# Softmax and memory denominators made by VectorE alone, in an attention and feed-forward kernel

## The chip, the cores and the metric

The kernel runs on one core of a Trainium2 chip. The metric is the device time of one execution in microseconds (us). A core has five engines with a queue of their own each, and each queue is worked off strictly in its order: TensorE (PE, with its weight loads as PEld), VectorE (DVE), ScalarE (ACT), GpSimd (POOL) and SyncE (SP, which issues the DMAs here). Engines wait for each other by semaphores.

## The reference

Four batches, eight heads, 576 rows, head size 64. Each head has causal softmax attention and a lookup in a memory matrix, mixed by a gate; the result goes through a feed-forward network with a rational activation.

```python
scores = scale * np.matmul(q, k.transpose(0, 1, 3, 2))      # causal mask, minus the row's maximum
a = np.exp(scores)
a /= a.sum(-1, keepdims=True) + 1e-09
local = np.matmul(a, v)
q_p = phi(q)                                   # phi(x) = x + 1 above zero, exp(x) below
mem_ret = np.einsum('bhsd,bhde->bhse', q_p, M_prev)
mem_norm = np.einsum('bhsd,bhd->bhs', q_p, z_prev)[..., None] + 1e-06
g = 1.0 / (1.0 + np.exp(-beta))[None, :, None, None]
attn_out = g * mem_ret / mem_norm + (1 - g) * local
# x = attn_out as [2304, 512]
h = x @ w_in                                   # 512 -> 2048
P = a0 + a1 * h + a2 * h**2 + a3 * h**3
Q = 1.0 + abs(b0) * abs(h) + abs(b1) * h**2
out = (P / (Q + 1e-6)) @ w_out                 # 2048 -> 512
```

The two weights arrive as 64-bit floats, everything else as 32-bit floats. The change concerns the two denominators: `sum + 1e-9` of the softmax and `phi(q).z + 1e-6` of the memory.

## The kernel before

The attention is cut into 16 units, one for each batch and pair of heads (`prep`, `scores`, `tile23`, `tail`, `av`). A unit has nine softmax tiles: for each of its two heads four of 128 rows with 128, 256, 384 and 512 keys, and one for the last 64 rows of both heads together, with 576 keys. The function `prob` (lines 697 to 724) makes one such tile: VectorE takes the row's maximum (L704), ScalarE the exponential with its row sum (L708), then the row sum is turned into a factor and the tile is scaled by it, and TensorE transposes it (`tr`, L503). The factor has the gate in it: `(sum + 1e-9) * 1/(1 - g)`, and then its reciprocal (L719). The tile called st holds the statistics of one softmax tile, one number for each row: columns for the maxima, the sums, the product and the reciprocal. The constants g1 and gtail hold 1/(1 - g).

In `prep` each unit makes phi(q) (the tile E), the product with z (written over nk), its sum over the head (den, 128 x 10, L655), and from it the factor `g / (phi(q).z + 1e-6)`, with which E is scaled (L662, recorded under the helper's L519 or L520). Here GpSimd adds 1e-6 (L657), VectorE takes the reciprocal (L658), and GpSimd or VectorE multiplies by g (the constant gt).

The feed-forward part takes 256 rows at a time and six of the sixteen blocks of the hidden width beside the attention, the other ten after it. Its chain `act_chain` runs on ScalarE, GpSimd and VectorE. The weights are split into a high and a low part on the three engines as well (L981 to L1000).

The order of all instructions is made ahead of time by a planner in the kernel's file (`Sched.place`). Each operation has a cost in nanoseconds for each engine that may do it; the planner repeatedly picks the operation that can start first by its own clock, with priorities to break ties, and where several engines may do an operation it takes the one with the smallest sum of start and cost. The costs are `c_pool`, `c_dve` and the like. A table RATE stretches an operation on VectorE or GpSimd while the other runs an operation of certain kinds (the letter at the end of an entry, "-" for none). So a cost that changes in one place moves instructions everywhere on all engines. The softmax factor had two choices:

```python
sc.op([("pool", c_pool(1, 1), lambda: G.tensor_scalar(...), "s"),          # L716
       ("dve", 130, lambda: V.tensor_scalar(...))],                        # L717
```

The planner put 90 of the 144 on GpSimd (L716) and 54 on VectorE (L717).

Of the kernel before, what the change touches and what calls it, by code (L numbers as in the profile page):

```python
# [15 lines left out]
ALU = mybir.AluOpType  # L16
# [28 lines left out]
def c_act(n, psum=True, ap=0):  # L45
    return (51 if psum else 93) + 0.833 * n + 93 * ap


def c_dve(n):
    return 69 + 1.042 * n  # L50


def c_dve1(n):
    return 69 + 0.64 * n


def c_pool(n, ap=0):
    return 161 + 0.833 * n + 83 * ap


def c_pool2(n):
    return 55 + 2.39 * n
# [254 lines left out]
def tile_attention_ffn(  # L317
# [15 lines left out]
    V, A, G, T, SY = nc.vector, nc.scalar, nc.gpsimd, nc.tensor, nc.sync  # L333
# [11 lines left out]
    sc = Sched()  # L345
# [27 lines left out]
    for i in range(2):  # L373
        r, r2 = slice(64 * i, 64 * i + 64), slice(64 - 64 * i, 128 - 64 * i)
# [9 lines left out]
    bt = const.tile([128, H], F32, name="bt")  # L384
    SY.dma_start(out=bt, in_=beta.partition_broadcast(128))
    gt = const.tile([128, H], F32, name="gt")
# [43 lines left out]
    for x in tags(atp, "qd", N["qd"], [128, 2, 128], F32R):  # L430
        for i in range(2):
            r = slice(64 * i, 64 * i + 64)
# [73 lines left out]
    def act(cost, fn, reads, writes, pri):  # L506
        return sc.op([("act", cost, fn)], reads, writes, pri)

    def dve(cost, fn, reads, writes, pri, kind="-"):
        return sc.op([("dve", cost, fn, kind)], reads, writes, pri)  # L510

    def pool(cost, fn, reads, writes, pri):
        return sc.op([("pool", cost, fn, "s")], reads, writes, pri)

    def tt(n, out, in0, in1, op, reads, writes, pri, engines=("pool", "dve")):

        def kw():
            return dict(out=out(), in0=in0(), in1=in1(), op=op)
        opts = {"pool": ("pool", c_pool2(n), lambda: G.tensor_tensor(**kw()), "t"),  # L519
                "dve": ("dve", c_dve(n), lambda: V.tensor_tensor(**kw()), "2")}  # L520
        return sc.op([opts[e] for e in engines], reads, writes, pri)
# [89 lines left out]
    def prep(u, p):  # L611
        bb, c = divmod(u, KC)
# [13 lines left out]
        for i in range(2):  # L626
            r = slice(64 * i, 64 * i + 64)
# [11 lines left out]
        for i in range(0 if d["direct"] else 2):  # L639
            o = d["qk"][i]  # L640
            r = slice(64 * i, 64 * i + 64)
# [6 lines left out]
        E, R, den = sc.buf("E"), nk, sc.buf("den")  # L648
# [5 lines left out]
           [(E, None), (zb, None)], [(R, None)], p)  # L654
        dve(c_dve(640), lambda: V.tensor_reduce(out=den.t, in_=R.t, axis=AX.X, op=ALU.add),  # L655
            [(R, None)], [(den, None)], p)
        pool(c_pool(10), lambda: G.tensor_scalar(den.t, den.t, 1.0, 1e-6, op0=ALU.mult, op1=ALU.add), [], [(den, None)], p)  # L657
        dve(140, lambda: V.reciprocal(den.t, den.t), [], [(den, None)], p)  # L658
        tt(10, lambda: den.t, lambda: den.t, lambda: gt[:, 2 * c:2 * c + 2].unsqueeze(1).to_broadcast([128, 5, 2]), ALU.mult,
           [], [(den, None)], p)  # L660

        tt(640, lambda: E.t, lambda: E.t, lambda: den.t.unsqueeze(3).to_broadcast([128, 5, 2, 64]), ALU.mult, [(den, None)], [(E, None)], p)  # L662

        bk, tf = bank(), bank()
# [32 lines left out]
    def prob(Pst, parts, gcol, n, p):  # L697

        P, st = Pst
        mx = len(parts) - 1  # L700
        for x, (bk, w, m, c0) in enumerate(parts):
            def f(bk=bk, w=w, m=m, x=x):
                s = bk.t[:, 0:w]
                V.tensor_tensor_reduce(out=s, in0=s, in1=m, scale=-0.125, scalar=st.t[:, 0:1] if x else 3.0e38,  # L704
                                       op0=ALU.add, op1=ALU.min, accum_out=st.t[:, x:x + 1])
            dve(c_dve(w) + 8, f, [(st, ("m", 0))] if x else [], [(bk, None), (st, ("m", x))], p)
        for x, (bk, w, m, c0) in enumerate(parts):
            act(c_act(w, ap=2), lambda bk=bk, w=w, x=x, c0=c0: A.activation(  # L708
                P.t[:, c0:c0 + w], bk.t[:, 0:w], AF.Exp, bias=st.t[:, mx:mx + 1], scale=-1.0, accum_out=st.t[:, 2 + x:3 + x]),
                [(bk, None), (st, ("m", mx))], [(P, x), (st, ("l", x))], p)  # L710
        l = slice(2, 3)
        if mx:
            l = slice(3, 4)
            dve(65, lambda: V.tensor_tensor(out=st.t[:, 3:4], in0=st.t[:, 2:3], in1=st.t[:, 3:4], op=ALU.add),
                [(st, ("l", 0))], [(st, ("l", 1))], p, "2")
        sc.op([("pool", c_pool(1, 1), lambda: G.tensor_scalar(st.t[:, 4:5], st.t[:, l], 1e-9, gcol, op0=ALU.add, op1=ALU.mult), "s"),  # L716
               ("dve", 130, lambda: V.tensor_scalar(st.t[:, 4:5], st.t[:, l], 1e-9, gcol, op0=ALU.add, op1=ALU.mult))],  # L717
              [(st, ("l", mx))], [(st, "r")], p)
        dve(75, lambda: V.reciprocal(st.t[:, 5:6], st.t[:, 4:5]), [(st, "r")], [(st, "i")], p)  # L719
        sc.op([("pool", c_pool(n, 1), lambda: G.tensor_scalar(P.t[:, 0:n], P.t[:, 0:n], st.t[:, 5:6], 0.0, op0=ALU.mult, op1=ALU.add), "s"),  # L720
               ("act", c_act(n, False, 1), lambda: A.activation(P.t[:, 0:n], P.t[:, 0:n], AF.Copy, scale=st.t[:, 5:6])),
               ("dve", c_dve1(n) + 61, lambda: V.tensor_scalar(P.t[:, 0:n], P.t[:, 0:n], st.t[:, 5:6], None, op0=ALU.mult), "1")],
              [(st, "i")], [(P, None)], p)
        return P

    def scores(u, i, t, p):
        bb, c = divmod(u, KC)
        d = ST[u]
        n = 128 * (t + 1)
        bk = bank()  # L730
        qs = slice(128 * t, 128 * t + 128)

        def f():
            if d["direct"]:
                r, x = slice(64 * i, 64 * i + 64), d["t"].t[:, 0:4 * SM].rearrange("p (a b) -> p a b", a=4)
                return [(x[r, a, qs], x[r, b, 0:n]) for a, b in ((1, 2), (1, 3), (0, 2))]
            x = d["qk"][i].t
            return [(x[:, 0, qs], x[:, 1 + b, 0:n]) for b in range(2)]
        m, src = (3, d["t"]) if d["direct"] else (2, d["qk"][i])
        P = probs(n)  # L740
        mm(lambda: [(bk.t[:, 0:n], a, b, x == 0, x == m - 1) for x, (a, b) in enumerate(f())], (6 if d["direct"] else 2) * c_mm(n),
           [(src, None)], [(bk, None)], p, take=P)
        return prob(P, [(bk, n, mk[:, 512 - 128 * t:640], 0)], g1[:, 2 * c + i:2 * c + i + 1], n, p)
# [43 lines left out]
    def tail(u, p):  # L787
# [12 lines left out]
        mm(lambda: f(s1, SM, 2 * SM, 3 * SM), 3 * c_mm(SM), [(t, None), (qd, None)], [(s1, None)], p, take=P)  # L800
        mm(lambda: f(s2, 64, 4 * SM, 4 * SM + 64), 3 * c_mm(64), [(t, None), (qd, None)], [(s2, None)], p)
        P = prob(P, [(s1, 512, mk[:, 0:512], 0), (s2, 64, mt, 512)], gtail[:, c:c + 1], S, p)
        pt, p2 = bank(), bank()
        tr(lambda: [(b4(pt)[:, x, :], P.t[:, 128 * j:128 * j + 128], idf) for x, j in enumerate((3, 0, 1, 2))], 4 * 109,
# [103 lines left out]
    pr = PRI  # L908
    load(0, -1)
    prep(0, 0)  # L910
    for u in range(U):
        base = 100.0 * u
        if u + 1 < U:
            load(u + 1, base + pr["load"])
        for i in range(2):
            tiles01(u, i, base + 10 + pr["head"] * i)
            av(u, i, 0, base + pr["av0"] + pr["head"] * i)
        if u + 1 < U:
            prep(u + 1, base + pr["prep"])
        for i in range(2):  # L920
            for t in range(2, 4):
                tile23(u, i, t, base + pr["t2"] + pr["head"] * i + 4 * (t - 2))
        tail(u, base + pr["tail"])
        for i in range(2):
            av(u, i, 1, base + pr["av1"] + i)
        spill(u, base + pr["av1"] + 2)
# [169 lines left out]
    for g in range(NG1):  # L1096
        t0 = 256 * g
        p = FP + pr["group"] * g
# [47 lines left out]
    for g in range(NG1 - turns + 1):  # L1146
        ts = [256 * x for x in (range(turns) if g == 0 else [g + turns - 1])]
        t0 = ts[0]
        p = FP2 + 5000 * (t0 // 256)
        ob = group(ts, list(range(F0, NF)), "h2", "o2", None, "xg2", p, pr["ahead2" if g < NG1 - turns else "last"])  # L1150
        for ti in range(2 * len(ts)):
            r = t0 + 128 * ti
# [68 lines left out]
```

## Time and profile before

| | us |
|---|---|
| three runs: lowest, median, highest | 733.32, 734.24, 737.19 |
| the profiled execution | 736.42 |
| its span, first to last instruction | 734.6 |

| engine | busy us | share of the span |
|---|---|---|
| TensorE | 664.3 | 90% |
| VectorE | 590.4 | 80% |
| ScalarE | 506.5 | 69% |
| GpSimd | 461.4 | 63% |

The attention's last softmax tile is scaled at about 360 us; after that only feed-forward work is left. The busy share is a mean over these two very different parts. A row of groups gives the busy time of all instructions of a line, operation and shape, the mean of one in ns, and the idle time of the engine in front of them. The chain of work is followed back from the last instruction to what released each step, so its pieces are the time on the path that ended last.

### The profile page before, as it was taken

Reading aid. Unit: us, or ns where it says so; the run is one execution under the profiler, and the core shown is the slowest. Engines: PE = TensorE matmul, PEld = TensorE weight load, DVE = VectorE, ACT = ScalarE, POOL = GpSimd, SP = SyncE. Lnnn points to the kernel's source line nnn. Section 1 sums busy time; section 2 is a strip of 40 time slices with the busy share of each in tenths; the row PEclk is TensorE's granted clock in tenths of the full one; section 3 lists DMA queues with packets and bytes.
Section 4 is the critical chain, followed back from the end, with each engine's and each line's share of the span. In section 5 each row is a group of like instructions: output and inputs, shape, how many; then the busy total and the mean of one; then the engine's idle time right before and its main releaser. Section 6 shows DMA issues by size and latency. Waiting matters only on the chain.

```text
span 734.6 us, 12896 instructions
## 1 busy us (share of the span) xinstructions
PE 664.3 (90%) x4113; PEld 578.9 (79%) x4113; DVE 590.4 (80%) x1371; ACT 506.5 (69%) x1121; POOL 461.4 (63%) x558
## 2 busy tenths in 40 slices
PE   3778788998989998889999999878899999999997
PEld 2656567887886777679889998767798998998996
DVE  5787877798999998789789999899775766657674
ACT  3756778789988899879666686575463854755762
POOL 3566656767765786656545887777753745645663
PEclk9999999999999999999999999999999999999999
DMA  6888687846679766764275443612342212212102
GB/s 152 178 202 216 138 204 180 235 112 191 157 168 236 188 162 157 219 159 104 80 260 161 169 159 106 242 61 87 116 124 91 72 62 83 87 58 72 45 9 79
DMA packets 102580, 102.56 MB, mean 140 GB/s; under 512 B 67632, under 2 KB 80432, under 8 KB 100208
## 3 DMA queue, kind: packets, MB, share of 16 engines
q1 hardware_dynamic: 102512, 101.73, 49.7%
q8 instruction: 33, 0.54, 0.3%
q14 instruction: 35, 0.29, 0.1%
HBM read 52.27 MB, written 23.59 MB: 103 GB/s over the span
## 4 chain that ended last, share of the span: by engine, by line
PE 51%; DVE 17%; ACT 11%; DMA 8%; issue 4%; POOL 4%; SPq 4%; DVEq 0%; ACTq 0%; POOLq 0%
PE bk L492 48%; SPq L485 4%; DMA xf<-in_moe_w_in_dram 3%; PE bk L503 3%; DVE bk L704 2%; ACT Ps L708 2%; DVE g L545 2%; ACT P L708 1%; DVE bk L525 1%; DVE gh L525 1%; ACT g L539 1%; DVE bk L987 1%; POOL tw L519 1%; DVE wa L983 1%; DVE wu L990 1%
## 5 line engine op out<-in xcount | busy, mean ns | idle before, releaser
L492 PEld LDWEIGHTS bk<-xg,w2i 128*128 128x128 f32 x1080 | 133.7, 193 | 6.5 <-DVE gl L1038 1.9
L492 PE MATMUL bk<-xg,w2i 128*128 128x256 f32 x1080 | 135.0, 284 | 3.3 <-DVE gl L1038 1.7
L492 PE MATMUL bk<-w2o,gh 128*128 128x512 f32 x360 | 113.3, 396 | 2.9 <-DVE gl L1038 2.9
L1014 ACT ACTIVATE ta<-bk 128x512 f32<-128x512 f32 x72 | 42.9, 596 | 86.7 <-PE bk L492 84.6
L1018 POOL TENSOR_SCALAR tw<-ta,cb 128x512 f32<-128x512 f32 x60 | 48.5, 808 | 83.5 <-ACT ta L1014 83.3
L519 POOL TENSOR_TENSOR tw<-tw,gh 128x512 f32<-128x512 f32 x54 | 70.6, 1307 | 40.6 <-DVE gh L525 39.6
L519 POOL TENSOR_TENSOR tw<-tw,ta 128x512 f32<-128x512 f32 x68 | 89.3, 1316 | 3.8 <-ACT tw L1019 0.3
L492 PE MATMUL bk<-xg,w1i 128*128 128x256 f32 x648 | 84.0, 284 | 0.2
L704 DVE CUSTOM_DVE_ANT_0 bk<-bk,mk 128x512 f32<-128x512 f32 (+3 forms) x144 | 72.7, 518 | 13.4 <-PE bk L492 11.9
L492 PEld LDWEIGHTS bk<-xg,w1i 128*128 128x128 f32 x648 | 80.9, 191 | 2.5 <-DVE g L545 0.8
L492 PEld LDWEIGHTS bk<-w2o,gh 128*128 128x128 f32 x360 | 67.1, 191 | 15.9 <-DVE gl L1038 3.1
L492 PE MATMUL bk<-w2o,gl 128*128 128x512 f32 x180 | 71.6, 398 | 5.7 <-DVE gl L1038 5.7
L1023 DVE TENSOR_TENSOR tb<-bk,tb 128x512 f32<-128x512 f32 x72 | 49.3, 684 | 33.0 <-ACT tb L1015 31.6
L1022 ACT ACTIVATE ta<-tw,lnb 128x512 f32<-128x512 f32 x72 | 52.0, 724 | 32.1 <-POOL tw L519 28.3
L492 PE MATMUL bk<-qk 128*128 128x128 f32 (+3 forms) x256 | 65.5, 360 | 4.3 <-DVE g L545 1.2
L492 PE MATMUL bk<-w1o,gh 128*128 128x512 f32 x216 | 68.7, 399 | 0.0
L525 DVE SCALAR_TENSOR_TENSOR gh<-bk,ca,ta 128x512 fp32r<-128x512 f32 x72 | 53.5, 743 | 18.4 <-ACT ta L1027 15.3
L525 DVE SCALAR_TENSOR_TENSOR bk<-bk,ca,tw 128x512 f32<-128x512 f32 x72 | 54.1, 751 | 14.4 <-POOL tw L519 13.9
L1015 ACT ACTIVATE tb<-bk,ca 128x512 f32<-128x512 f32 x72 | 55.7, 775 | 0.1
L1025 DVE SCALAR_TENSOR_TENSOR bk<-tb,ca,bk 128x512 f32<-128x512 f32 x72 | 53.8, 748 | 1.9 <-ACT ta L1014 1.0
L716 POOL TENSOR_SCALAR st<-st,g 128x1 f32<-128x1 f32 x78 | 24.0, 308 | 48.7 <-ACT Ps L708 41.4
L708 ACT ACTIVATE Ps<-bk,st 128x128 f32<-128x128 f32 (+2 forms) x96 | 46.0, 483 | 10.9 <-DVE st L704 8.1
(152 smaller groups left out, 1623.4 us busy)
## 6 DMA issues: line engine op xcount, KB each, us to landing
qk<-tt SPq DMA_DIRECT2D x32, 384.0 KB, 4.8
xh<-xg SPq DMA_DIRECT2D x9, 1024.0 KB, 4.7
xg<-xh SPq DMA_DIRECT2D x9, 1024.0 KB, 4.8
xf<-in_moe_w_in_dram SPq DMA_DIRECT2D x16, 512.0 KB, 4.4
qk<-tt SPq DMA_DIRECT2D x32, 256.0 KB, 3.6
xf<-in_moe_w_out_dram SPq DMA_DIRECT2D x16, 512.0 KB, 4.8
xs<-x SPq DMA_DIRECT2D x16, 288.0 KB, 2.7
xf<-xs SPq DMA_DIRECT2D x9, 512.0 KB, 5.8
```

What stands on the lines that cost most here:

```text
L485: SY.dma_start(out=o, in_=i)
L492: T.matmul(o, lhsT=l, rhs=r, start=s0, stop=s1, skip_group_check=more)
L519: opts = {"pool": ("pool", c_pool2(n), lambda: G.tensor_tensor(**kw()), "t"), "dve": ("dve", c_dve(n), lambda: V.tensor_tensor(**kw()), "2")}
L525: return dve(c_dve(n) + 61 * ap, lambda: V.scalar_tensor_tensor(out=out(), in0=in0(), scalar=scalar() if callable(scalar) else scalar, in1 ...
L704: V.tensor_tensor_reduce(out=s, in0=s, in1=m, scale=-0.125, scalar=st.t[:, 0:1] if x else 3.0e38, op0=ALU.add, op1=ALU.min, accum_out=st.t ...
L708: act(c_act(w, ap=2), lambda bk=bk, w=w, x=x, c0=c0: A.activation(P.t[:, c0:c0 + w], bk.t[:, 0:w], AF.Exp, bias=st.t[:, mx:mx + 1], scale= ...
L1014: act(c_act(N), lambda: A.activation(a_(), h(), AF.Abs), [(hb, None)], [(ta, None)], p)
L1015: sc.op([("act", c_act(N, ap=2), lambda: A.activation(b_(), h(), AF.Identity, scale=ca[:, 3:4], bias=ca[:, 2:3])), ("dve", c_dve(N) + 61, ...
L1018: sc.op([("pool", c_pool(N, 2), lambda: G.tensor_scalar(w_(), a_(), cb[:, 1:2], cb[:, 0:1], op0=ALU.mult, op1=ALU.add), "s"), ("act", c_ac ...
L1022: act(c_act(N, False, 1), lambda: A.activation(a_(), w_(), AF.Ln, scale=2.0 ** -63, bias=lnb[:, 0:1]), [(tw, None)], [(ta, None)], p)
L1023: dve(c_dve(N), lambda: V.tensor_tensor(out=b_(), in0=h(), in1=b_(), op=ALU.mult), [(hb, None)], [(tb, None)], p)
L1025: dve(c_dve(N) + 61, lambda: V.scalar_tensor_tensor(out=h(), in0=b_(), scalar=ca[:, 1:2], in1=h(), op0=ALU.add, op1=ALU.mult), [(tb, None) ...
```

## The change

Both denominators become one VectorE operation of the form (a + constant) * b, where b is a second tile: 1/(1 - g) for the softmax, and for the memory the constant bt, which holds 1/g. The multiplication by g after the reciprocal falls away. GpSimd has no part in either. In the planner the operation costs 75 ns for the softmax and 90 ns for the memory, of kind "-".

```diff
-        pool(c_pool(10), lambda: G.tensor_scalar(den.t, den.t, 1.0, 1e-6, op0=ALU.mult, op1=ALU.add), [], [(den, None)], p)
+        dve(90, lambda: V.scalar_tensor_tensor(
+            out=den.t, in0=den.t, scalar=1e-6, in1=bt[:, 2 * c:2 * c + 2].unsqueeze(1).to_broadcast([128, 5, 2]), op0=ALU.add,
+            op1=ALU.mult), [], [(den, None)], p)
         dve(140, lambda: V.reciprocal(den.t, den.t), [], [(den, None)], p)
-        tt(10, lambda: den.t, lambda: den.t, lambda: gt[:, 2 * c:2 * c + 2].unsqueeze(1).to_broadcast([128, 5, 2]), ALU.mult,
-           [], [(den, None)], p)
...
-        sc.op([("pool", c_pool(1, 1), lambda: G.tensor_scalar(st.t[:, 4:5], st.t[:, l], 1e-9, gcol, op0=ALU.add, op1=ALU.mult), "s"),
-               ("dve", 130, lambda: V.tensor_scalar(st.t[:, 4:5], st.t[:, l], 1e-9, gcol, op0=ALU.add, op1=ALU.mult))],
-              [(st, ("l", mx))], [(st, "r")], p)
+        dve(75, lambda: V.scalar_tensor_tensor(out=st.t[:, 4:5], in0=st.t[:, l], scalar=1e-9, in1=gcol, op0=ALU.add, op1=ALU.mult),
+            [(st, ("l", mx))], [(st, "r")], p)
```

In the changed file the softmax's operation stands on L715, its reciprocal on L717, the memory's operation on L657 and its reciprocal on L660; the scaling on GpSimd is L718, the maximum L703. TensorE has the same 4040 matrix instructions in both orders, VectorE 1481 instructions in place of 1373, GpSimd 450 in place of 563, ScalarE 952 in place of 963.

The first place is GpSimd's queue in the first unit, from the product with z (nk) on. Before:

```order
L519 TENSOR_TENSOR nk_129<-E_155,zb_154 128x640
L657 TENSOR_SCALAR den_156<-den_156 128x10
L519 TENSOR_TENSOR den_156<-den_156,gt 128x10
L519 TENSOR_TENSOR E_155<-E_155,den_156 128x640
L716 TENSOR_SCALAR st_164<-st_164,gtail 128x1
L720 TENSOR_SCALAR P_157<-P_157,st_164 128x576
L531 TENSOR_SCALAR w1i_187<-tw_217 128x512
```

And with the change (P and Ps are softmax tiles, w1i a weight's high part):

```order
L519 TENSOR_TENSOR nk_129<-E_155,zb_154 128x640
L519 TENSOR_TENSOR E_155<-E_155,den_156 128x640
L531 TENSOR_SCALAR w1i_187<-tw_217 128x512
L519 TENSOR_TENSOR w1i_193<-tw_217,w1i_187 128x512
L718 TENSOR_SCALAR Ps_162<-Ps_162,st_166 128x256
```

The three small operations on den and st are gone from GpSimd, and the scaling of this first tile went to ScalarE.

The second place is VectorE's queue in the eleventh unit, from the sum of den (L655) on, at about 230 us of the trace before. Before:

```order
L655 TENSOR_REDUCE den_156<-nk_129 128x10
L719 RECIPROCAL st_167<-st_167 128x1
L704 ISA bk_120,st_164<-bk_120,mk 128x512
L704 ISA st_164 128x1
L658 RECIPROCAL den_156<-den_156 128x10
L719 RECIPROCAL st_168<-st_168 128x1
L520 TENSOR_TENSOR den_156<-den_156,gt 128x10
L704 ISA bk_124,st_166<-bk_124,mk 128x512
L704 ISA st_166 128x1
L719 RECIPROCAL st_169<-st_169 128x1
L717 TENSOR_SCALAR st_164<-st_164,g_100 128x1
```

With the change:

```order
L655 TENSOR_REDUCE den_156<-nk_129 128x10
L715 SCALAR_TENSOR_TENSOR st_170<-st_170,g_100 128x1
L715 SCALAR_TENSOR_TENSOR st_169<-st_169,g_100 128x1
L657 SCALAR_TENSOR_TENSOR den_156<-den_156,bt 128x10
L717 RECIPROCAL st_170<-st_170 128x1
L717 RECIPROCAL st_169<-st_169 128x1
L660 RECIPROCAL den_156<-den_156 128x10
L703 ISA bk_122,st_168<-bk_122,mk 128x512
L703 ISA st_168 128x1
L525 SCALAR_TENSOR_TENSOR bk_126<-bk_126,ca,tw_218 128x512
```

Three of the new operations stand in front of three reciprocals, and the next tile's maximum (bk_122) stands behind all six.

The third place is GpSimd's queue at the same point. Before:

```order
L519 TENSOR_TENSOR nk_129<-E_155,zb_154 128x640
L716 TENSOR_SCALAR st_167<-st_167,g_100 128x1
L716 TENSOR_SCALAR st_168<-st_168,g_100 128x1
L657 TENSOR_SCALAR den_156<-den_156 128x10
L720 TENSOR_SCALAR Ps_163<-Ps_163,st_167 128x384
L716 TENSOR_SCALAR st_169<-st_169,g_100 128x1
L720 TENSOR_SCALAR P_157<-P_157,st_168 128x512
L519 TENSOR_TENSOR E_155<-E_155,den_156 128x640
```

With the change:

```order
L519 TENSOR_TENSOR nk_129<-E_155,zb_154 128x640
L718 TENSOR_SCALAR Ps_162<-Ps_162,st_167 128x256
L718 TENSOR_SCALAR P_157<-P_157,st_170 128x512
L718 TENSOR_SCALAR P_158<-P_158,st_169 128x512
L519 TENSOR_TENSOR E_155<-E_155,den_156 128x640
L519 TENSOR_TENSOR tw_217<-tw_217,ta_211 128x512
```

The small operations between the wide ones are gone; a wide operation follows a wide one.

## Rows read from the trace of the kernel before

**Rows 1.** The page: busy us of each engine, then the chain's shares.
```profile
PE 664.3 (90%) x4113; PEld 578.9 (79%) x4113; DVE 590.4 (80%) x1371; ACT 506.5 (69%) x1121; POOL 461.4 (63%) x558
PE 51%; DVE 17%; ACT 11%; DMA 8%; issue 4%; POOL 4%; SPq 4%; DVEq 0%; ACTq 0%; POOLq 0%
```

**Rows 2.** Busy time in stretches: stretch, its length, then each engine's busy us.
```profile
core 0: us, PE busy (x) PEld busy (x) DVE busy (x) ACT busy (x) POOL busy (x), PEclk, DMA share, GB/s
...
150.00:300.00 150.00, 136.26 (x892) 116.78 (x892) 137.86 (x420) 134.47 (x360) 103.18 (x150) 0.98 0.69 172
...
360.00:550.00 190.00, 178.17 (x1108) 159.72 (x1107) 168.91 (x250) 116.77 (x189) 130.96 (x121) 0.98 0.43 148
```

**Rows 3.** What TensorE waited for: us in total, times, longest us.
```profile
PE bk L492 <- DVE gl L1038: 10.3, 5, 2.9
PE bk L503 <- POOL Ps L720: 7.7, 7, 2.0
...
PE bk L503 <- POOL E L519: 4.6, 2, 4.2
```

**Rows 4.** Groups by shape on GpSimd: count, busy us, mean ns, idle before.
```profile
L716 POOL TENSOR_SCALAR st<-st,g 128x1 f32<-128x1 f32 x78 | 24.0, 308 | 48.7 <-ACT Ps L708 41.4 <-ACT P L708 2.3 <-DMA qk<-tt 0.8
...
L657 POOL TENSOR_SCALAR den<-den 128x10 f32<-128x10 f32 x16 | 3.4, 210 | 5.0 <-DVE den L655 2.3 <-DVE st L719 1.8
L716 POOL TENSOR_SCALAR st<-st,gtail 128x1 f32<-128x1 f32 x12 | 3.2, 264 | 11.0 <-DVE st L714 10.7
...
L519 POOL TENSOR_TENSOR den<-den,gt 128x10 f32<-128x10 f32 x11 | 2.4, 221 | 2.2 <-DVE den L658 1.2 <-DVE st L719 0.8
```

**Rows 5.** Groups by shape on VectorE.
```profile
L525 DVE SCALAR_TENSOR_TENSOR bk<-bk,ca,tw 128x512 f32<-128x512 f32 x72 | 54.1, 751 | 14.4 <-POOL tw L519 13.9
...
L525 DVE SCALAR_TENSOR_TENSOR tw<-tw,gh 128x512 f32<-128x512 f32 x18 | 17.0, 948 | 0.1
...
L717 DVE TENSOR_SCALAR st<-st,g 128x1 f32<-128x1 f32 x50 | 10.0, 206 | 3.6 <-ACT Ps L708 2.3 <-ACT P L708 0.7
...
L714 DVE TENSOR_TENSOR st<-st 128x1 f32<-128x1 f32 x16 | 5.6, 348 | 1.4 <-ACT P L708 1.3
...
L520 DVE TENSOR_TENSOR den<-den,gt 128x10 f32<-128x10 f32 x5 | 2.3, 453 | 0.0
```

**Rows 6.** Lines L714 and L717: ns of the shortest, median and longest.
```profile
L714 DVE TENSOR_TENSOR st<-st x16: 142/159/1206, 18.2 to 344.0; 128x1 f32<-128x1 f32 x16
...
L717 DVE TENSOR_SCALAR st<-st,g x50: 187/205/216, 20.5 to 357.4; 128x1 f32<-128x1 f32 x50
```

**Rows 7.** Order of time near 281 us: start us, duration us, engine, operation.
```profile
281.30 1.27 POOL L519 TENSOR_TENSOR ms<-mn,ms 128x512 fp32r<-128x512 f32 x1
...
281.50 1.09 DVE L714 TENSOR_TENSOR st<-st 128x1 f32<-128x1 f32 x1
```

**Rows 8.** Pieces of the chain that ended last: start us, us, what.
```profile
31.59 0.23 DVE st L717 x2
...
54.29 0.36 POOL st L716
54.66 0.11 issue
...
258.41 0.66 DVE st L714
...
281.57 1.02 DVE st L714
...
313.21 0.21 DVE st L717
...
347.67 0.27 POOL st L716
```

**Rows 9.** Groups by shape on VectorE that the planner moves.
```profile
L722 DVE TENSOR_SCALAR Ps<-Ps,st 128x384 f32<-128x384 f32 x2 | 2.9, 1426 | 0.0
...
L520 DVE TENSOR_TENSOR w2o<-wu,w2o 128x512 fp32r<-128x512 f32 x1 | 1.8, 1783 | 0.0
```

## The prediction

> **What bounds the kernel now.** I read the page's busy shares and chain first, then the busy time by stretches, then TensorE's waits, then the groups of the small operations that the change touches. TensorE is busy 664.3 us of 734.6 and makes 51% of the chain that ended last; VectorE is second with 17%, GpSimd has 4% [rows 1]. So time is lost where TensorE waits, and the engine most often waited for is VectorE, not the one that is relieved. The mean hides the middle of the attention: from 150 to 300 us VectorE is busy 137.86 of 150 us, more than TensorE (136.26), while GpSimd has 103.18 [rows 2]. VectorE has 12.1 us to spare there, GpSimd 46.8. The change puts work on the fuller of the two. What speaks for it is that TensorE waits 7.7 us for scaled softmax tiles and 4.6 us for the scaled E, both from GpSimd [rows 3], behind chains that cross between the engines.
>
> **The change part by part.** *Removed.* GpSimd loses 78 and 12 operations of L716, 16 of L657 and 11 products with gt: 24.0 + 3.2 + 3.4 + 2.4 = 33.0 us of busy time [rows 4]. Most of it costs nothing today, since GpSimd has room. On the path lie eight pieces of L716, 2.6 us together (the first 0.36, the last 0.27 us [rows 8]), and three pieces on den, 0.21, 0.22 and 0.34 us, 0.8 together, near their groups' means [rows 4]. With each of these eleven goes one crossing between engines, 0.11 us by the piece after the first [rows 8], 1.2 us in all. VectorE loses 54 operations of L717, of which 13 lie on the path in twelve pieces, 2.0 us together (first 0.23 for two, last 0.21) [rows 8]. What goes from the path: 2.6 + 0.8 + 1.2 + 2.0 = 6.6 us.
>
> *Added.* VectorE gets 144 + 16 = 160 operations with two tiles in SBUF as inputs, and the order shows that none stays on GpSimd. No row of before has this operation at 128x1. The nearest is L714: same tile st, same size, right behind the same row sum, also two inputs in SBUF. Undisturbed it takes 142 to 159 ns, but its longest takes 1206 and its mean is 348 [rows 5, 6]. L717, which takes the gate as a scalar for each row and reads one tile, never takes more than 216 ns in 50 [rows 6]. The difference is a wait for GpSimd: one L714 starts at 281.50 us while GpSimd is inside an operation of 1.27 us begun at 281.30, and ends at 282.59, within 0.02 us of GpSimd's end [rows 7]. That the new form of operation suffers the same way is seen at a larger size: with both inputs in SBUF (tw, gh) it has a mean of 948 ns, with one in PSUM (bk) 751, though the number of elements is the same [rows 5]. 948 - 751 = 197 ns and 348 - 159 = 189 ns: two operations, one price, 0.19 us a piece in the mean.
>
> The Trainium skill, SBUF — State Buffer, section Who interferes with whom, says that a VectorE instruction with two SBUF inputs contends with a GpSimd instruction that reads SBUF, and that whichever came second is blocked until the first has finished, while one with at most one SBUF input outside the two-port modes is free of it. By that rule all 160 new operations are exposed and the 54 replaced ones were not; the rows on L714 and L717 agree. Without the rule one could hold the new 128x1 form for an operation like L717, and the sum would then be the lower bound below.
>
> *What of it lies on the path.* Two of the 16 L714 lie on the chain, with 0.66 and 1.02 us [rows 8]: 1.68 / 16 = 0.105 us of path per operation. 160 x 0.105 = 16.8 us. The sum: 16.8 - 6.6 = +10.2 us. From below: if the new operation never waited and came on the path as L717 does, 2.0 / 54 = 0.037 us each, it would be 5.9 - 6.6 = -0.7 us. From above: the product on den, L520, also with two inputs in SBUF, has a mean of 453 ns [rows 5], a stall of 294 in place of 189; 16.8 x 294 / 189 = 26.1, and the sum is +19.5 us. I take +10, since L714 is the nearer row by place, size and count.
>
> *Does VectorE have room?* A second account, from 150 to 300 us. The nine softmax tiles and one den of each of 16 units lie between 15 and 360 us, so about 160 x 150 / 345 = 70 new operations fall there. Back to back two L717 take 0.23 us [rows 8], 0.115 each; with the stall a new one holds the queue 0.115 + 0.19 = 0.305 us, 70 make 21.4 us. 54 x 150 / 345 = 23 of L717 go, 2.7 us. The net 18.7 us do not fit in the 12.1 us that VectorE has idle [rows 2]; at least 6.6 us overflow even if it never waited for anything. That is the same size as the sum over the path, by another way.
>
> Behind a stalled operation waits the whole queue of VectorE: its own reciprocal, thus GpSimd's scaling and TensorE's transpose; the next tile's maximum, thus ScalarE's exponential; the subtractions that TensorE's second product needs. The planner prices the operation at 75 ns and lets nothing stretch it, so it doesn't plan around the stall. GpSimd's queue loses its small operations and stands with wide ones back to back (third place of the order), so that a new operation meets one more often, not less.
>
> *Moved.* The new plan gives VectorE five more scalings of softmax tiles (10 to 15; one of 128x384 costs 1426 ns [rows 9]) and takes two splits of the feed-forward's input; for the attention part I call that even, 0 to +4 us, and it is in the range. After it, VectorE gets four more weight subtractions at 1.78 us [rows 9], 7.1 us, from 360 to 550 us, where it is busy 168.91 of 190 [rows 2] and TensorE already waits 10.3 us for gl [rows 3]. Its 21 us of room cover that, if they fall beside a wait; if not, up to 7 us come on top. I count 0. TensorE's work is the same 4040 instructions.
>
> The profiled execution took 736.42 us (734.6 of span and 1.8 around it), 2.2 above the median of the three runs. 736.4 + 10.2 = 746.6 against its own time, and 734.2 + 10.2 = 744.4 against the median. I forecast 744.
>
> **The rivals.** *Faster, the shorter chain wins.* Before, an L716 also stood behind whatever GpSimd was doing; the stall is then the old wait in another queue, and in exchange an operation and two crossings go from 90 of 144 chains. For it: GpSimd waited 41.4 us in front of L716 for the row sums [rows 4], so it often was free when the new operation would run. Price: the GpSimd pieces and crossings, 4.6 us, and of TensorE's nine waits of 12.3 us [rows 3] some 0.25 us each, 2.3 us: 727 to 730 us. Against it: GpSimd's wait held no one else's work, VectorE's does, and VectorE is the fuller. It wins if the new operation's mean stays under some 0.2 us.
>
> *No change.* The stalls come, but half of them where VectorE would have waited anyway: 16.8 / 2 - 6.6 = +1.8 us, 736 us. For it: over the whole attention VectorE is not as full as in its middle. Against it: the chain runs through L714 at the rate used.
>
> *Slower still.* The attention overflows and the four weight subtractions come late as well: 744 + 7 = 751, and with the upper price 754 to 761 us. It would show as more waiting for gl between 360 and 550 us.
>
> **How the numbers follow.** The forecast, 738 to 750 us, has 0.45; slower still 0.15; no change 0.2; faster 0.2. Half a percent, 3.7 us, is about what a measurement of this kernel can tell from no change, so slower has 0.6, the same 0.2, faster 0.2. The range from 728 to 757 leaves out about half of the faster case's lower end and the top of the worst one. The likeliest case's own range is 738 to 750.
>
> **What would show it.** Right: L715 with a mean near 350 ns and a longest above 1 us, ending where a GpSimd operation ends; VectorE's busy time up by some 40 us and above 140 of 150 us between 150 and 300; GpSimd's down by about 30; the end of the softmax later than 360 us; TensorE's idle time growing there. Wrong: L715 never above 250 ns (then no stall, and at most 734 us); or stalls as priced, with the softmax ending at 360 us or before, which would say that the chain had more room than its pieces show; or a loss that arises after the softmax, which would be the moved weight work.

## The result and the profile after

The changed kernel takes 740.3 us in the median of seven runs (737.16 to 744.62), against 733.36 for seven of the kernel before: a ratio of 1.0103, 95% interval 1.0077 to 1.0128. By the ratio that is 7.6 us slower (5.6 to 9.4), where 10 had been forecast; the two medians are 6.9 us apart. TensorE's granted clock (the share of its full speed that the chip granted) does not differ in the mean: 0.980 in these seven runs, and 0.980 in eleven runs of the kernel before beside the first experiments. The profiled execution took 743.18 us, 741.4 of it span.

The page of the changed kernel, as [rows 1]: busy time of each engine, then the chain's shares.

```profile
PE 668.1 (90%) x4113; PEld 578.4 (78%) x4113; DVE 608.6 (82%) x1479; ACT 500.6 (68%) x1110; POOL 426.8 (58%) x445
...
PE 52%; DVE 24%; DMA 8%; ACT 7%; issue 4%; SPq 3%; POOL 2%; DVEq 0%; ACTq 0%; POOLq 0%
```

GpSimd lost 34.6 us of busy time (33.0 in the prediction), VectorE gained 18.2 (some 40 in the prediction). VectorE's share of the chain rose from 17 to 24%, GpSimd's halved. The same two stretches of the changed kernel as in [rows 2]:

```profile
150.00:300.00 150.00, 134.63 (x872) 113.40 (x870) 137.95 (x445) 128.10 (x345) 86.81 (x97) 0.98 0.69 171
...
360.00:550.00 190.00, 176.95 (x1088) 157.50 (x1089) 166.35 (x261) 113.00 (x189) 125.31 (x119) 0.97 0.41 142
```

From 150 to 300 us VectorE is no busier than before (137.95 and 137.86), though it does 445 instructions there in place of 420; TensorE does 872 in place of 892. VectorE's gain lies elsewhere, most of it from 20 to 150 us (110.45 in place of 100.10 us busy). That the work did not fit in the middle and went later is a reading; the experiments below test it. The second product of the attention (the tile vs) is its last step; the rows give shortest, median and longest ns, then the first and last start in us, of the kernel before and then of the changed one:

```profile
L492 PE MATMUL bk<-g,vs x286: 213/307/614, 137.3 to 364.9; 128*128 128x320 f32 x66, 128*128 128x256 f32 x44, 128*128 128x192 f32 x22, 128*128 128x64 f32 x11
```
```profile
L492 PE MATMUL bk<-g,vs x286: 213/307/614, 140.2 to 373.3; 128*128 128x320 f32 x66, 128*128 128x256 f32 x42, 128*128 128x192 f32 x22, 128*128 128x64 f32 x11
```

The attention ends 8.4 us later. The new operations, in the form of [rows 6] (two rows of L715, one of L657):

```profile
L715 DVE SCALAR_TENSOR_TENSOR st<-st,g x128: 93/154/1290, 21.5 to 368.9; 128x1 f32<-128x1 f32 x128
L715 DVE SCALAR_TENSOR_TENSOR st<-st,gtail x16: 137/148/1268, 20.1 to 349.5; 128x1 f32<-128x1 f32 x16
...
L657 DVE SCALAR_TENSOR_TENSOR den<-den,bt x16: 150/160/606, 14.9 to 339.1; 128x10 f32<-128x10 f32 x16
```

The stall is there, up to 1290 ns where 154 is the median. In order of time near 119 us (start, duration), as [rows 7]:

```profile
118.70 1.54 POOL L519 TENSOR_TENSOR nk<-E,zb 128x640 f32<-128x640 f32 x1 [0.82 <-PE bk L492]
118.97 1.29 DVE L715 SCALAR_TENSOR_TENSOR st<-st,g 128x1 f32<-128x1 f32 x1
```

VectorE's operation ends at 120.26, GpSimd's at 120.24. Of the 144 operations on st, 30 took over 180 ns, and each of these ends 3 to 22 ns after the end of a GpSimd operation. But fewer are hit than L714 had suggested, as the groups by shape show:

```profile
L715 DVE SCALAR_TENSOR_TENSOR st<-st,g 128x1 f32<-128x1 f32 x128 | 32.8, 262 | 6.0 <-ACT Ps L707 4.4 <-ACT P L707 0.9
...
L715 DVE SCALAR_TENSOR_TENSOR st<-st,gtail 128x1 f32<-128x1 f32 x16 | 3.7, 233 | 0.0
```

The mean of all 144 is 258 ns, so some 0.10 us of stall each. (Busy time counts records that overlap once, so 36.5 us is a little less than 144 means.) On the chain L715 has 1.6% of the span, 11.9 us (the header of the chain, by line):

```profile
by line: PE bk L492 48.4%; issue 4.3%; DVE bk L703 3.2%; PE bk L503 3.1%; SPq L485 2.7%; DVE g L545 2.5%; DMA xf<-in_moe_w_in_dram 2.1%; DVE st L715 1.6%; DVE E L525 1.4%; DMA vz<-in_v_dram 1.4%; DMA qk<-tt 1.3%; ACT Ps L707 1.3%; DVE bk L5
```

### The profile page after: what moved, and what is told of

Read it like the earlier page. It is cut to its first block, busy times and chain, and to the rows that moved or that the text cites. A ratio compares the mean times of both kernels' runs of the same rounds, so it can differ in the third digit from the quotient of the medians.

```text
span 741.4 us, 12922 instructions
## 1 busy us (share of the span) xinstructions
PE 668.1 (90%) x4113; PEld 578.4 (78%) x4113; DVE 608.6 (82%) x1479; ACT 500.6 (68%) x1110; POOL 426.8 (58%) x445
## 4 chain that ended last, share of the span: by engine, by line
PE 52%; DVE 24%; DMA 8%; ACT 7%; issue 4%; SPq 3%; POOL 2%; DVEq 0%; ACTq 0%; POOLq 0%
PE bk L492 48%; DVE bk L703 3%; PE bk L503 3%; SPq L485 3%; DVE g L545 2%; DMA xf<-in_moe_w_in_dram 2%; DVE st L715 2%; DVE E L525 1%; DMA vz<-in_v_dram 1%; DMA qk<-tt 1%; ACT Ps L707 1%; DVE bk L525 1%; DVE gh L525 1%; DVE tb L1021 1%; DVE gl L1036 1%
## 5 line engine op out<-in xcount | busy, mean ns | idle before, releaser
L718 POOL TENSOR_SCALAR Ps<-Ps,st 128x128 f32<-128x128 f32 (+2 forms) x72 | 36.8, 513 | 101.3 <-DVE st L717 42.7
L703 DVE CUSTOM_DVE_ANT_0 bk<-bk,mk 128x512 f32<-128x512 f32 (+3 forms) x144 | 73.0, 515 | 6.7 <-PE bk L492 6.1
L492 PEld LDWEIGHTS bk<-w2o,gh 128*128 128x128 f32 x360 | 66.6, 191 | 13.7 <-DVE gh L525 1.3
L492 PE MATMUL bk<-qk 128*128 128x256 f32 (+3 forms) x256 | 68.4, 369 | 6.3 <-DVE g L545 1.9
L525 DVE SCALAR_TENSOR_TENSOR gh<-bk,ca,ta 128x512 fp32r<-128x512 f32 x72 | 53.6, 744 | 16.1 <-ACT ta L1025 15.5
```

Of the source, the lines that this page charges most:

```text
L492: T.matmul(o, lhsT=l, rhs=r, start=s0, stop=s1, skip_group_check=more)
L525: return dve(c_dve(n) + 61 * ap, lambda: V.scalar_tensor_tensor(out=out(), in0=in0(), scalar=scalar() if callable(scalar) else scalar, in1 ...
```

## The experiments

All times are medians; ratios are to the kernel before on the same chip. "The old order" is the planner's order of the kernel before, "the new order" that of the changed kernel. Where an order is kept, all instructions but those on st and den stand as they were on every engine.

**The stall taken away, new order.**

```diff
-V.scalar_tensor_tensor(out=st.t[:, 4:5], in0=st.t[:, l], scalar=1e-9, in1=gcol, op0=ALU.add, op1=ALU.mult)
+V.tensor_scalar(st.t[:, 4:5], st.t[:, l], 1e-9, gcol, op0=ALU.add, op1=ALU.mult)
```

> The order of the changed kernel, instruction by instruction on every engine; only the softmax's 144 operations on L715 take the gate as a scalar for each row (the form of L717 before, one SBUF tensor input, 205 ns, never stalled in 50) in place of as a second tile (154 ns median, but 30 of 144 stalled, mean 258). Theory stalls: the 15.6 us of stalls go, 144 x 0.05 us of own length come back in part; the time falls from 740 to 733 to 737, the line's longest is under 0.25 us. Rival plan (the new order alone costs the 7 us): 740 within 2. Rival load (90 more operations on VectorE cost it, stalled or not): 741 to 744, since each is longer.

Measured 742.96 us, ratio 1.0117 (1.0072 to 1.0161). The stalls on st are gone:

```profile
L715 DVE TENSOR_SCALAR st<-st,g x128: 152/205/217, 20.4 to 365.6; 128x1 f32<-128x1 f32 x128
```

The time isn't. The two ratios differ by 0.0014, about 1 us, with some 4 us of uncertainty either way: the gain of 3 to 7 us that the stall theory wanted is not there. The form without a stall is 50 ns longer each time, and 16 products on den still have two inputs, so this is no clean removal; but in this order the stalls on st alone do not explain the loss.

**The new operations in the old order.** The planner sees the costs and engines of before; at its places VectorE does the new operations.

```diff
-("pool", c_pool(1, 1), lambda: G.tensor_scalar(..., 1e-9, gcol, ...), "s")
+("pool", c_pool(1, 1), lambda: V.scalar_tensor_tensor(..., scalar=1e-9, in1=gcol, ...), "s")
...
-pool(c_pool(10), lambda: G.tensor_scalar(den.t, den.t, 1.0, 1e-6, ...), ...)
+pool(c_pool(10), lambda: V.scalar_tensor_tensor(out=den.t, in0=den.t, scalar=1e-6, in1=bt[...], ...), ...)
```

> The order planned for the kernel before (same places, same costs for the planner), but at those places VectorE does the new operations: 144 on st and 16 on den with two SBUF inputs; GpSimd does none of them. Theory stalls: as in the changed kernel some 30 of 160 meet a GpSimd operation and the time rises from 733 to 738 to 743. Rival plan: 733 within 2, or below by the chain's shorter hop (729 to 733). Rival load: 736 to 742 even with few stalls (mean under 0.2 us).

Measured 740.95 us, ratio 1.0094 (1.0059 to 1.0129): the operations alone cost as much as the whole change. Where they stall is telling. In this file L718 are the places that the planner had given to VectorE, L717 those it had given to GpSimd:

```profile
L718 DVE SCALAR_TENSOR_TENSOR st<-st,g 128x1 f32<-128x1 f32 x50 | 24.9, 500 | 3.2 <-ACT Ps L709 2.3 <-ACT P L709 0.2
...
L717 DVE SCALAR_TENSOR_TENSOR st<-st,g 128x1 f32<-128x1 f32 x78 | 16.7, 223 | 0.7 <-ACT Ps L709 0.3
```

500 ns against 223: the planner had chosen VectorE where it had GpSimd busy, and there the operation with two SBUF inputs waits more. Over all 144 places 43 took over 180 ns, and 42 of these end 1 to 20 ns after the end of a GpSimd operation.

**The load alone, and den alone, in the old order.** First, VectorE does all 144 products in L717's form, with no stall; den is untouched:

```diff
-("pool", c_pool(1, 1), lambda: G.tensor_scalar(st.t[:, 4:5], st.t[:, l], 1e-9, gcol, ...), "s")
+("pool", c_pool(1, 1), lambda: V.tensor_scalar(st.t[:, 4:5], st.t[:, l], 1e-9, gcol, ...), "s")
```

> The order of the kernel before; the softmax's product stands at the same 144 places, but VectorE does all of them in L717's form, with the gate as a scalar for each row (one SBUF tensor input, no stall); den is untouched. Theory stalls: no stall, so 731 to 736. Theory load (VectorE can't take 90 more short operations, stalled or not): 737 to 742, as with the new operations in this order (740.95). Theory plan (only a re-plan costs): 733.

Measured 735.41 us, ratio 1.0023 (0.9996 to 1.0049). Second, the new den alone, at the old places:

> The order of the kernel before; the softmax is untouched, den is made by VectorE's new operation at the places where GpSimd stood, and the product with the gate is gone. The same instructions as in the run with the new den alone (745.15), but in the old order. Theory plan: 731 to 735, so that the re-plan of that run cost its 11 us. Theory operations: 740 to 746.

Measured 734.9 us, ratio 1.0022 (0.9996 to 1.0048). The row of the first:

```profile
L716 DVE TENSOR_SCALAR st<-st,g 128x1 f32<-128x1 f32 x78 | 15.2, 205 | 2.9 <-ACT Ps L708 1.9 <-ACT P L708 0.8
```

Ninety more operations of 205 ns each on VectorE cost 1.7 us, which can't be told from nothing. So in the old order it is the form with two inputs that costs: 1.0094 - 1.0023 = 0.7%, about 5 us, give or take 3. Some 1.6 us of it may belong to den (at most 3.5 by that run's interval).

**The new den alone, planned anew.** The change's first half, softmax as before.

> The memory's denominator as in the change, the softmax's as before; a new order is planned. Theory stalls: 16 operations, in the changed kernel 1.1 us of stall in all, against two GpSimd operations fewer on each of 16 chains: 730 to 735. Rival plan: any re-plan moves the time by several us either way, so that 16 small operations could give 728 to 742.

Measured 745.15 us, ratio 1.0157 (1.0123 to 1.0191). The same operations in the old order took 734.9. Ten us are the order's.

**Honest costs for the planner.** `dve(75, ...)` becomes `dve(155, ..., "2")`, `dve(90, ...)` becomes `dve(160, ..., "2")`.

> The changed kernel with the planner told 155 and 160 ns in place of 75 and 90 and that the operation is of the kind that GpSimd's wide operations stretch; the instructions are the same kinds, the order is planned anew. Theory stalls: the planner can only place other work around them, so most stalls stay, 735 to 741. Rival plan: the order was bad because it was planned on wrong costs, so 728 to 735.

Measured 747.56 us, ratio 1.0196 (1.016 to 1.0233): slower than both ranges. Telling the planner the operation's undisturbed duration and its kind did not make the order better.

**Two draws with the operations of before.** One planner number is changed, no operation.

```diff
-dve(75, lambda: V.reciprocal(st.t[:, 5:6], st.t[:, 4:5]), ...)
+dve(80, lambda: V.reciprocal(st.t[:, 5:6], st.t[:, 4:5]), ...)
```

> The kernel before with one number in the planner changed: the softmax's reciprocal is priced at 80 ns in place of 75. The operations are those of before; only the order (and which engine does an operation where there is a choice) is planned anew. Theory plan: the old order is a good draw, and this one is slower by 4 to 12 us (738 to 746). Theory operations: 731 to 736.

> The kernel before with another number changed: GpSimd's small operation on den is priced 5 ns higher. Otherwise as the run with the reciprocal at 80 ns, for a second draw of an order. Theory plan: 738 to 746. Theory operations: 731 to 736.

Measured 751.98 us, ratio 1.0276 (1.0244 to 1.0309), and 753.77 us, ratio 1.0287 (1.0258 to 1.0316). Five nanoseconds in a table cost some 20 us, more than the change. Their attentions end when that of before does (the first, then the second):

```profile
L492 PE MATMUL bk<-g,vs x286: 213/306/522, 140.4 to 365.3; 128*128 128x320 f32 x66, 128*128 128x256 f32 x44, 128*128 128x192 f32 x22, 128*128 128x64 f32 x11
```
```profile
L492 PE MATMUL bk<-g,vs x286: 213/307/615, 135.8 to 363.7; 128*128 128x320 f32 x66, 128*128 128x256 f32 x44, 128*128 128x192 f32 x22, 128*128 128x64 f32 x11
```

What differs is in the order: 279 and 273 feed-forward multiplications stand before the attention's last one, where before has 381 and the changed kernel 405. After the attention TensorE needs 0.155 us for one (65.22 us for 421 in the chain of the kernel before), so a hundred fewer are 15.5 us left for later. Is that number the cause?

**Draws chosen by that number.** The operations of before with the reciprocal at 78 ns (528 of them), and those of the changed kernel with the product at 110 ns (468).

> The kernel before, operations and all, with the softmax's reciprocal priced at 78 ns for the planner: another draw of the order. It was chosen because 528 feed-forward multiplications stand in TensorE's queue before the attention's last one, where before has 381, the two draws at 752 and 754 us 279 and 273. If that number decides and the attention's end stays at 362 to 374 us as in all traces so far, 147 x 0.155 us less is left after it: 710 to 725. If the attention only ends later for it, since TensorE has the same work and the same idle time: 733 to 755, as any other draw.

> The changed kernel with its softmax product priced at 110 ns in place of 75: a draw of the order with 468 feed-forward multiplications before the attention's last one (the changed kernel has 405). If that number decides: 724 to 733. If any draw lands where it will: 735 to 755.

Measured 736.13 us, ratio 1.0054 (1.002 to 1.0087), and 755.45 us, ratio 1.0303 (1.0261 to 1.0345). The number alone does not decide. In the first draw the attention just ends later:

```profile
L492 PE MATMUL bk<-g,vs x286: 213/306/399, 139.1 to 378.6; 128*128 128x320 f32 x66, 128*128 128x256 f32 x44, 128*128 128x192 f32 x22, 128*128 128x64 f32 x11
```

The end of the attention and the work done by then go together into one account, and only a run gives the first. From the start of the attention's last multiplication to the end of the span, twelve of the fourteen profiled executions took 0.166 to 0.168 us for each feed-forward multiplication that was left of 2592. In the draws at 752 and 754 us 102 and 108 more were left when the attention ended at its old time: that gives 17 and 18 us of their 19 and 21. The changed kernel's attention ended 8.4 us later with 24 fewer left, which is 4 us less. With the new operations in the old order it ended 7.3 us later (372.2) with the same number left.

Only the two draws chosen by the number took more for each, 0.173 and 0.172 us. In the first of them the same stretch as in [rows 2] reads:

```profile
360.00:550.00 190.00, 174.78 (x1055) 156.88 (x1054) 168.42 (x264) 114.65 (x195) 129.84 (x126) 0.93 0.40 140
```

By the account this draw should be 11 us faster than before (147 x 0.167 = 24.6 us less left, 13.7 us later); its profiled execution was 0.9 us slower (735.5 us of span in place of 734.6). TensorE stood idle 15.2 us in this stretch in place of 11.8, and its mean granted clock was 0.93 in place of 0.98, more of the time at 1.2 GHz, the lower of its two levels, in place of 2.4. By estimate the clock takes up to 190 x 0.05 / 0.98 = 10 us. Over all runs it was 0.969 with this draw and 0.981 in the kernel before beside it.

**GpSimd's operations in the new order.** The converse of the second experiment: the changed kernel's order, with GpSimd doing all 144 products and den's addition and product.

```diff
-dve(75, lambda: V.scalar_tensor_tensor(out=st.t[:, 4:5], in0=st.t[:, l], scalar=1e-9, in1=gcol, ...), ...)
+dve(75, lambda: G.tensor_scalar(st.t[:, 4:5], st.t[:, l], 1e-9, gcol, op0=ALU.add, op1=ALU.mult), ...)
```

> The order planned for the changed kernel, but at its places GpSimd does the softmax's product (all 144, the form of L716) and, on den, the addition and the product with the gate behind the reciprocal, as before the change. Nothing of the denominators' sums is left on VectorE, so no stall and no load there. Theory order (the changed kernel is slower by its order): 738 to 744. Theory operations (stall and load on VectorE): 731 to 736. If it is above 745, the new order needs the products early and GpSimd's queue is too late for them.

Measured 748.77 us, ratio 1.0217 (1.0178 to 1.0255): neither. GpSimd's way is 8 us worse than the new operations in this order (in the kernel before VectorE did 54 of the 144, so these are not quite its operations). VectorE's waits show why (us, times, longest):

```profile
DVE st L716 <- POOL st L714: 29.8, 56, 2.5
```

The reciprocals stand close behind the products there, and VectorE waits 29.8 us for GpSimd; in the kernel before it was 5.4 us in 11 waits. Here the order fits the operations that it was planned for, and the change of both can't be split into two numbers that add.

**The product done twice, new order.**

```diff
-dve(75, lambda: V.scalar_tensor_tensor(...), ...)
+dve(75, lambda: [V.scalar_tensor_tensor(...) for _ in range(2)], ...)
```

> The changed kernel in its order, with each of the 144 products of the softmax done twice by VectorE (the second writes the same numbers). Theory stalls or load on VectorE: the second copy adds some 0.1 us each and a second chance of a stall, so 5 to 10 us more than the changed kernel, 745 to 751. If the new order has room for it on VectorE: 740 within 3, and the products can't be what makes it slower.

Measured 765.23 us, ratio 1.045 (1.0411 to 1.049): 25 us more than the changed kernel, far over the 5 to 10 expected. The groups of L715, and the middle stretch:

```profile
L715 DVE SCALAR_TENSOR_TENSOR st<-st,g 128x1 f32<-128x1 f32 x256 | 66.0, 261 | 7.1 <-ACT Ps L707 1.4 <-ACT P L707 0.9
...
L715 DVE SCALAR_TENSOR_TENSOR st<-st,gtail 128x1 f32<-128x1 f32 x32 | 6.0, 186 | 0.6
```
```profile
150.00:300.00 150.00, 128.91 (x804) 107.26 (x803) 139.87 (x471) 122.05 (x322) 79.61 (x89) 0.93 0.64 159
```

L715 is busy 72.0 us in place of 36.5; all of VectorE is busy 633.9 us in place of 608.6, since its other operations took less and some records overlap. These 25.3 us more became 25 us of time. On the chain L715 has 38.5 us in place of 11.9. So what is added to these products in the new order comes on the path nearly whole. VectorE is still no fuller than 139.87 of 150 us in the middle; TensorE does 804 instructions there in place of 872.

| order | operations | ratio |
|---|---|---|
| old | of before; one input on VectorE; new den; all new | 1; 1.0023; 1.0022; 1.0094 |
| new | all new; one input on st; on GpSimd; doubled | 1.0103; 1.0117; 1.0217; 1.045 |
| other draws | of before | 1.0276; 1.0287; 1.0054 |
| other draws | new den; all new, honest costs; all new, 110 ns | 1.0157; 1.0196; 1.0303 |

## Why the prediction was right, and where its reasons were not

*The direction and the size* held: 740.3 us lies inside the likeliest case's 738 to 750.

*The mechanism of the stall* held: two SBUF inputs, up to 1290 ns, ended by GpSimd's end. Its share of the loss is shown in the old order, 6.9 us with two inputs against 1.7 with one. In the new order it is not shown: taking it from st gave no time back.

*The price of the stall* was too high: 0.19 us a piece was put, 0.10 measured in the new order and 0.16 in the old one. Of L714's 16 samples six took over 180 ns, and three waits of 0.6 us and more made the mean; of 144 new operations 30 took over 180 ns. By these few samples a GpSimd operation was met less often, not more: the sentence about wide ones back to back was wrong. GpSimd without its small operations is busy 86.81 us from 150 to 300 in place of 103.18. The second source of the price, 948 - 751 = 197 ns, compared two different forms. The row of 948 ns has a median of its own:

```profile
L525 DVE SCALAR_TENSOR_TENSOR tw<-tw,gh x18: 672/679/1785, 152.3 to 407.5; 128x512 f32<-128x512 f32 x18
```

By it the stall there is 948 - 679 = 269 ns, so that the two prices agreed was chance.

*The sum of the path* was 16.8 - 6.6 = +10.2 us. On the chain the new operations have 11.9 us (L715) and 1.0 (L657). What goes is 7.0, since VectorE's own products on den, 0.4 us of the chain (L520), had been left out. That makes +5.9. The first experiment warns against reading it as the cause: its L715 has 6.9 us on its chain, 5 less, and no less time. The rival "faster" was also priced a little low: TensorE waited another 4.9 us for scaled tiles from GpSimd (P, L720, five times), which [rows 3] lacks.

*The account of VectorE's room* is not shown. The signs are there: VectorE's busy time from 150 to 300 us did not rise, TensorE did fewer instructions, and the attention ended 8.4 us later. But the old order with the one-input form, which lost nothing that can be measured, has VectorE as busy there and with more instructions (452 in place of the changed kernel's 445):

```profile
150.00:300.00 150.00, 133.95 (x884) 114.47 (x884) 139.53 (x452) 133.22 (x357) 89.85 (x108) 0.99 0.71 177
```

And the draw with the reciprocal at 80 ns has far fewer TensorE instructions (804 in place of 872) with VectorE less busy:

```profile
150.00:300.00 150.00, 126.63 (x804) 107.42 (x803) 130.48 (x413) 123.67 (x343) 97.44 (x146) 0.95 0.70 168
```

So neither a full VectorE nor fewer TensorE instructions in a stretch proves by itself that VectorE's load is what costs.

*The signs.* Right were the longest above 1 us, the end with GpSimd's, GpSimd's fall by about 30 us (34.6) and the softmax's end after 360 us (the last L715 starts at 368.9). Wrong were the mean of 350 ns (258), VectorE's 40 us more (18.2) and above 140 in the middle (137.95). TensorE's idle time there grew only from 13.7 to 15.4 us. TensorE waited 6.6 us for gl in place of 10.3, so the sign of "slower still" did not come.

*The step without ground* is "Moved": the re-plan was put at 0 to +4 us in the attention and up to 7 behind it, as a handful of operations that change engine, and counted as 0. In this draw that came true: with the new operations the old order has 1.0094 and the new one 1.0103, no difference that the runs can tell. But six orders drawn besides the changed kernel's, three of them with the operations of before, came out from +0.5 to +3.0%, 4 to 22 us, all slower than before. A term of that size had no part in the sum. So the agreement of 10 with 7.6 us is in part luck: with the product at 110 in place of 75 ns in the planner the same change was 22 us slower, at the upper end of the range.

*Open.* How much of the 7.6 us is the order's and how much the operations' is not settled, and may have no answer: the operations alone, in the old order, give 6.9, the new order with all products on GpSimd gives 16. The slower draws were followed to the account of the attention's end and the work left then, but not to the waits that made either.

## What to carry to other kernels

Where a planner sets the order of the whole program, a changed cost is a new draw, and a draw can weigh more than the change. Time a draw with the old operations and one perturbed number before crediting or blaming an edit, and try the new operations in the old order. Of each draw read when the stage with the waits ends and how much of the other work is done by then. Before giving VectorE a second SBUF input beside a busy GpSimd, look for a row of the same size that has it, and read its longest beside its median; a number for each row passed as a scalar costs 50 ns more here and never waited in 144.

## What the runs showed of the hardware

A 128x1 operation of VectorE with two SBUF inputs took 154 ns in the median and up to 1290; the same product with one SBUF tensor input and a scalar for each row took 205 and at most 217 in 144. In the run with the new operations in the old order the first form's mean was 500 ns at places planned while GpSimd was busy and 223 at the others. Of the changed kernel's 144 operations of the first form, the 30 that took over 180 ns all ended 3 to 22 ns after a GpSimd operation; of the 144 of the second form in its order, 35 ran wholly inside a GpSimd operation. VectorE's busy time from 150 to 300 us was 137.86 in the kernel before and 137.95 to 140.35 in the five of its order or the new one in which VectorE made all the softmax's products, whether its busy time over the run rose by 6.2 or by 43.5 us; in four other draws it was 127.6 to 131.4.
